# Last tokens' values by head in DRAM, their late output products moved, and a new instruction order, in a segment-recurrent attention kernel on Trainium2

## The chip, the cores and the metric

One Trainium2 chip, one of its cores. The metric is the device time of one execution in microseconds (us). The times before are 831.28, 831.71 and 833.63 us, median 831.71. Where a profile is read, it is one execution of the same program, recorded by the hardware profiler. The engines are named as the profile names them: PE is TensorE's matrix multiply, PEld its loading of weights (the stationary operand), DVE is VectorE, ACT ScalarE, POOL GpSimd, and SP the SyncE queue from which nearly all DMAs are issued.

## What is computed

Two attentions over the same 2048 tokens of width 512, mixed by a gate for each token. Branch A is recurrent: 64 segments of 32 tokens, each with 8 memory tokens ahead of it. The output of the memory rows of one segment is the memory of the next, so the 64 segments run strictly one after the other. Branch B has 32 heads of width 16, works in four blocks of 512 tokens and carries a state of keys and values from block to block.

```python
x, mem = A_x, A_mem0                        # [1,2048,512], [1,8,512]
for s in range(64):                         # branch A: H=32 heads, Dh=128
    h = concat([mem, x[:, 32*s:32*s+32]])   # 40 rows
    q, k, v = h @ Wq, h @ Wk, h @ Wv        # [32 heads, 40, 128] each
    p = softmax(where(mask, q @ k.T * 128**-0.5, -1e9))
    o = (p @ v) @ Wo                        # [40, 512]
    mem, a[s] = o[:8], o[8:]
b = infini_attention(x, B_wq, B_wk, B_wv, B_beta) @ B_wo
g = sigmoid(sum(x * gate_w))
out = g * a + (1 - g) * b
```

The mask lets every row see the memory and makes the 32 tokens causal. Therefore the last 8 of the 40 rows of a segment (the "last tokens", 24 to 31 of the segment) are seen by themselves alone. Neither their keys, queries and values nor their output products are on the way from one memory to the next.

## The kernel before

**The segment.** A tile of PE has 32 columns, so a segment's own work is done on 32 rows: the 24 first tokens and the 8 memory rows (`hT`, line 1420 fills the tokens, line 1317 the memory that the segment before left). Function `p_seg` issues, for each half `r` of 16 heads: the projections of q, k and v (`wproj`, its matmuls are line 1389), ScalarE or VectorE copies to SBUF, VectorE transposes in blocks of 32 x 32 (line 1445), the scores (1460), the exponentials, their sums (1483), the product with the values (1525), and the output product (`wo`, 1294) with a fold (1018) that gives the next segment's memory. Everything here hangs together in one chain, segment after segment.

**The last tokens.** The last 8 tokens of four segments make 32 rows together. Function `p_rest(j, kind, r)` projects them for four segments at once (`j` is a block of four segments, 0 to 15; six calls for each block). Their columns of `x` are gathered by POOL into `xr` (1342). Keys and queries are transposed by VectorE into `rem_k` and `rem_q` (1375). The values go through a staging buffer (`stg`, three of them in rotation, function `stage`) to DRAM (`rest_v`, line 1361, a row for each token), and `p_restload(s)` (1398) loads those of one segment into one of two buffers `rem_v`, so that a row of SBUF is a pair (head, token). They are used at line 1464 (keys and queries) and 1530 (the values, as a second part of the product 1525). Block 0 is brought to `rem_v` of segment 0 without DRAM, by a product with a matrix of ones and zeros, `spread`, which POOL makes at the start (lines 836 to 840).

**Late output products.** POOL collects the last tokens' attention outputs of four segments in `OTr` (1547), and function `p_orest(t)` multiplies them by `Wo` with the same `wo` (64 matmuls, eight groups of eight). Its result is stored as rows of `a_rows` in DRAM (1336). Function `p_tail(t)` loads 128 rows of `a_rows` (1267), adds branch B's output and stores the final rows (1279).

**Order.** All operations are created by functions that are called in the order of the keys given in `build` (`self.at(key, function, ...)`; a key of 52.3 is a little past segment 52). They are not issued in that order: `schedule` takes each engine's order word for word from the string `ORDER`, a compressed list of operation numbers for each of the five queues. The costs, loads and priorities in the calls were inputs of a planner that made this list. In the run they set only which PSUM banks are taken and which waits are left out as already implied. The waits themselves come from the reads and writes that each operation names (`reads`, `writes`), and each engine's queue is executed strictly in its order, so that an instruction that waits holds all behind it on its queue.

**Filler.** PE has nothing to do in many short moments of a segment's chain. The list puts there the matmuls that are not on the chain: the last tokens' projections and output products, branch B's projections, scores and values (1018, 1020, 1135, 1176), and the tails.

Of the kernel before, what the change touches and what calls it, by code (L numbers as in the profile page):

```python
# [8 lines left out]
ALU = mybir.AluOpType  # L9
AX = mybir.AxisListType  # L10
BF16 = mybir.dt.bfloat16
# [4 lines left out]
    "c-nPY2S8KT*FQHe$;%F5h*kvzgbJb-5f`;p+*<joRjYMxZCyxl*MZ_*EzVYL>#joGC_|-gl!_Mj!cn)N5E3BCecydA$;*3*pGr(#&OP^x-}#+$FT*v;w-P1BriC&|)l9G%"  # L16
    "s$dCNl9$dfOo!y$%Sq*U<KU-})t}r8g~OH`5C_L0IlpH{Zu60ErpZ%g?|dY)mVT8r{rR6&vufWz0XKitmNmTt@P2wmR^2Dcv_w$7^?_AAz2AA8e7FAFuxaq+6CJZ&>$@K7"
    "a`k4x;LhK`u7Fl2*3K}h-;zZ^CGUMQ3XHlb2NF6~pIm$7M7L^4SqPBZuB&lQes&dBOrNhbr&M-&?RW0{Gyur@9Aej5r1c*9z9FCBQ<MKYZ@AFnO|$d=EApZWoA|!<F)Pex"
    "qW?}XSAf!V?>@AKphu9`f7hJ7Uz&ji?#~&3*5!qbgAiq-=}NlHV5Lt-f!cbxIb3LaLi+iQZvQz&p|AIbJwvoMnT=8t&6;urZ7Elz{s9VecvjtqW{67b&Fei3-H%&F6RrAk"
    "jfrfpmX>0r1j@0$wIHITxRVJKaJ305d8}I2<rw+De-%R1j=?mTL2cAqEYPeVx*+<d_3sM{d94!w)=s1{WEMn~`p}h{>VJqxg;%LsZM+|HA3n{i^Rzw49p?HUNO*Z60pv2X"  # L20
    "%;xvh4-oZUFL|e`fYN=lZr6Dl8~`tP*J{I>Nlypld0Av;>O;_@;19Y=cme@NLy5M`zhX5&(w-+Nycz!jL<SydZ=;a5eCYy{7CsQUYA}u4u6+DSAArAjz1aZqIa@9vna$=`"
    "1v6&rsCP<}a>)dZs$${%eOq#QW3NG6NI~@0VWl>i%uGbfq)NI(Q~vvC3Z|q<P7;Z3Y{(qO0zBzlq-4Wj_(0D{m3`2C@G^rm^vVlpbgc`(!#$Sayy}eMeKw6Ic#&CT7QZTz"
    "IZ#m4lF<t49zer?>n)$T2y*jz-}(XU4sDueMhI!m+G-iR*CR7j00rLfewsz|o?ZJM@{G+aHi|M>t@0|<gJAHgG^y6kEC-PPP6S*A1lHd5d2t|svepYkTWoS|CCICZHxI*Y"
    "cOhy$BpevA7GNr`dSPU6)UL=u1ZV_2viD#pQJ7UW3Bcxw*54=amd;7h|1yb<tlojf($&)!lhv#NG{3nVs^p+zeb<wf$OI~>#kwYO<?M=;FwNyoje{-x4h|xCrPTLB(B1o8"
    "rEh^iMSZKO5#(1(4DdO(?~-X;{L4P1Y#941!K+QXew?W!pv$2OLy5*}(!kB0#M67kj5)mOspMx__uP6m>Qub?gRb?|j$klL%1KR-kVHV?&ZW0_YxBuZQ~mZaB>G4Vq;TjG"
    "P#_?t$X&L2lb<&|&gn?(iN1$W<5dlVnK;IVsO8lrmopaKB}*IL<Ai55?lbcMhg3>|BxP&n&7DYgZqz5$NLNMyJm<st8^GWZ!=Nu4QI-lOE=@Q<LPj<RWpg+a_dA617F^r`"
    "KlMr)MpgNgQk1sNgW!T_cxJ9(12*=LN4{@rSN=s1M`-8TlAU%;^-DO`PtQ@u7pEUUu+h6&CMoldd2P-BEvdK#ZSrC`c%N(wFr!^AEXuf?&Shi8c%Y?Vky_*>x)1&{8{C|?"
# [12 lines left out]
    "%dXODUOAuG7fA4=vs*KFmVzv9SVeY~QI#}jv1H?@mL!F`mKRwU3L{DFsQ2QfHrbXTUUG>=Y9@PHX`+43&xG12WN~OW(n___S4El^>#7`5rqf7Mo^lX*t(a~12-sD67?nXF"  # L40
    "q;r_W0z#d9E4ST48|6@BX-rN(#CA11y|B^Hu}cBr!MKPB6@LnL6B-szNL`%Vl5ITBm{sbDHe*B1W!463>&qlZ`V-6GP8IDmlt@YNs3CX^w_}My2Sz>7eiF|>2?x2%u{lv9"
    "Tzg=KQA4I<o!tf%(QNCU#p*8gVo{QoC{dSvnY@As+zC6`f{U<zPk*dFgr_2I9T#Lv<+@p*{tNtvP}>GsXa_WCl1UAP{cJKWJ**Mocc2+64&~y9aL8jTwdUC>iK;x(?jolw"
    "_zoMy<1m_Qq;@Y!(h%I(l}W}7ulF^bK5ENTW;f>HL@Xnb*aHjB4}B1P*Q-iT7FMXN3WU{3u~Rx^v!R~0meWSF8PA08C>;ke;yL@k*qp_eBZ5Uui4g}OkpRcnEZjg@pTLmy"
    "hh)eCH$Ic#0M+jPGTS@7Gx($;aKkSy#hgbU3{G_^3yHcZTl;09SN@bE;|hY*V3ttX&r!vk{!NMH>$lPyMmTj5K&g!l>|S%VASEW`ltZ#D_KH_o<L6v02R|dqy|CI9L!yeH"
    "z8B0GNO5Jv8A}R5tuef<L1|k28DNJ1=k|sE$iC1KXLT6O7nB{*$MA5<4rmsrB%+$*ILQGw9h(UvLt~l+{Q_9TDq_K<@um1Guz*|@_tMv?xEA{WVYGDe-sh_?NSm1?|LRIB"
    "^)c4`xK<zfpM8&%=gsM;9_esn^3(Bvi?1VJ!R_#2TglOC{JQb$G7n!cDd()18aXs65E{kKIG=ibkiHz$zYZ{`|CHH{hU3?7r0TDdPW#4E>s@`&-S^cML5NQ&w5U)Jf>9fD"
    "zA!uw3M{^OJDk2Z@`S2$SzUsDjCAl;E0-2VgMN=sH*?NVi-g9=Y6y8G#aClA2tH9ftjEf&nqZ(PsUG$YR}iGzwhZ;gcY7C6SDFX!MDY{XW{+2yZ->iJn_L5Jkru-1K3=6Y"
    "WqLEFu>qfLL*0s;6W2Sv_nDWy8>$K-Dhwuh;f}<Gv%)c5em3-8!SWm39tO%Q)Oa4O!ih_0>ihK<JLSYT1dAFI1s1vVR6I=W)C+=1(23Ej6M>q#=Gm+PJJWlq`gB)xeM<V7"
    "Z4P|hB5^Hl|8paYGz&VNK)uXIvo@s9i916q{x9Orr&4HhcFr2;mj?>74Ac~q`B)S+P2<-EzJ%JkN-RfhvkVtoN%4Zs&vT&h<`e`?D`^?RHZ4V0--upzyYcMbv^_J1wQYO^"
    "(<T~CTH%c)(yT7YU!XqlCqVMDALOts(Q966wSx3E+S^Kzt?~8=7In2!51|V3nJl{u?eMAAY6#oW{Nfw%$8C3CPFLKBpnq6`d#|s5{ZqMg;m(eKsQ>KJ6w51+0uIH7ez%&Y"  # L50
    "{{Aw2!=Mjv2x@!-#Hb}n28%lJJ5sh07~9k~_|M-UksgPx$NKH<``zc@orKA>pqsLmA}w|K<@F<e9dWz`nFukSy39aAD%F3VbF)drJ+s2r-~}EI@P{Rj9Ix8n{S5uJr=PZM"
# [12 lines left out]
    "WF>cwF#&(zB7X+6FKI7kY#lUq<8Lsq`pU}hTJP#HWM@Cg-roO9-<Q=c*R&Dee$uTk%v6_k+!O?x4jX@_18@Eq-+taNud9kT1$7-Tpj{1lRq=`Ru#IavEUl9idis5j_<Eys"
# [517 lines left out]
class Kernel:  # L582
# [1007 lines left out]
```

## Time and profile before

| | before |
|---|---|
| median of 3 runs | 831.71 us (831.28 to 833.63) |
| the profiled execution, device time | 832.18 us |
| its span, first to last instruction | 830.2 us |
| granted TensorE clock | 1.000 |
| loads of `rem_v` (line 1398) | 63 of 64 KB, issue 585 ns, landing 2.9 us (medians) |
| stores of `rest_v` (line 1361) | 28 of 128 KB from SP, 4 from ACT, issue 536 ns (SP, median) |
| VectorE transposes of last tokens (line 1375) | 64, 0.69 us each |

A line of the profile's list of groups gives line, engine, operation, output and inputs with their shapes, then the number of instructions, their busy time in us with the mean of one in ns, and the idle time of the engine just ahead of them with what ended it. In the table by stretches the columns are the stretch, its length, and for each engine the busy time with the number of instructions, then the granted clock, the mean share of the DMA engines, and GB/s. In the list of waits the three numbers are us in total, times, and the longest one. A line that begins with SPq is an instruction of the SP queue; its time is that of the issue, not of the transfer.

### The profile page before, as it was taken

The numbers are of one execution on the slowest core, as the hardware profiler recorded it, in microseconds if no ns is written. First come the engines' busy times: TensorE is split into PE (matmuls) and PEld (weight loads), VectorE is DVE, ScalarE is ACT, GpSimd is POOL, SyncE is SP. The second block draws the span as 40 slices with busy tenths as digits, with TensorE's granted clock in tenths as the row PEclk, the third lists the DMA queues.
The fourth block names the chain that finished last, engine by engine and source line by source line (L and its number), as shares of the span: only waits on it lengthen the run. The fifth ranks groups of instructions, "written<-read, shape, count | busy, mean of one in ns | idle before, by whom it ended". The sixth has DMA issues, their size and how long they took to land.

```text
span 830.2 us, 53252 instructions
## 1 busy us (share of the span) xinstructions
PE 805.0 (97%) x24462; PEld 520.7 (63%) x24462; DVE 623.3 (75%) x1417; ACT 557.7 (67%) x1264; POOL 256.8 (31%) x572
## 2 busy tenths in 40 slices
PE   8999999999999999999999999999999999998988
PEld 4446666666566666666666666666666666665655
DVE  4878667778778778677787787777777867777776
ACT  3667666777667766667666767677677666666663
POOL 3453221333232323322322422423313314333240
PEclk9999999999999999999999999999999999999999
DMA  9983101111111110211012111101111100001001
GB/s 345 412 249 61 45 17 39 39 45 23 47 27 28 39 26 19 50 34 44 25 39 43 39 27 32 41 18 32 32 36 33 40 25 12 21 19 26 10 22 36
DMA packets 71700, 45.62 MB, mean 55 GB/s; under 512 B 50046, under 2 KB 69942, under 8 KB 69942
## 3 DMA queue, kind: packets, MB, share of 16 engines
q1 hardware_dynamic: 70422, 41.18, 17.2%
q8 instruction: 192, 3.15, 1.6%
q10 hardware_dynamic: 1056, 1.05, 0.4%
q14 instruction: 30, 0.25, 0.1%
HBM read 30.72 MB, written 8.87 MB: 48 GB/s over the span
## 4 chain that ended last, share of the span: by engine, by line
PE 82%; DMA 6%; DVE 4%; ACT 4%; SPq 2%; issue 1%; POOL 0%; DVEq 0%; POOLq 0%
PE pb L1389 45%; PE pb L1294 16%; PE pb L1018 7%; DMA Wo_sb<-in_A_Wo_dram 4%; PE pb L1135 3%; PE pb L1525 3%; PE pb L1020 2%; PE pb L1176 2%; PE pb L1483 2%; PE pb L1460 1%; SPq L891 1%; DMA rest_v<-stg 1%; DMA wqB_sb<-in_B_wq_dram 1%; PE pb L1224 1%; ACT rc_sb L1489 1%
## 5 line engine op out<-in xcount | busy, mean ns | idle before, releaser
L995 ACT ACTIVATE st<-pb 128x512 bf16<-128x512 f32 (+2 forms) x309 | 147.0, 495 | 115.8 <-PE pb L1389 96.4
L1153 ACT ACTIVATE PTB<-pb 128x640 bf16<-128x640 f32 x240 | 159.3, 703 | 46.3 <-PE pb L1135 37.3
L1389 PE MATMUL pb<-Wv_sb,hT 128*32 128x512 bf16 x2048 | 160.0, 379 | 0.0
L1389 PE MATMUL pb<-Wq_sb,hT 128*32 128x256 bf16 (+1 forms) x3072 | 139.0, 308 | 0.4 <-DVE hT L1317 0.4
L1389 PE MATMUL pb<-Wk_sb,hT 128*32 128x512 bf16 x2048 | 134.1, 379 | 0.7 <-DVE phiK L1204 0.7
L1294 PE MATMUL pb<-Wo_sb,OT_sb 128*32 128x256 bf16 x4096 | 130.7, 273 | 1.3 <-issue 0.8
L1294 PEld LDWEIGHTS pb<-Wo_sb,OT_sb 128*32 128x32 bf16 x4096 | 101.3, 96 | 14.3 <-ACT OT_sb L995 2.2
L1389 PEld LDWEIGHTS pb<-Wq_sb,hT 128*32 128x32 bf16 x3072 | 83.6, 97 | 41.1 <-issue 1.1
L1159 POOL TENSOR_SCALAR_AFFINE_SELECT PTB<-PTB 128x512 bf16<-128x512 bf16 x120 | 77.0, 642 | 95.6 <-ACT PTB L1153 89.2
L1445 DVE STREAM_TRANSPOSE QT_sb<-st 128x256 bf16<-128x256 bf16 (+1 forms) x192 | 94.1, 508 | 9.2 <-ACT st L995 7.4
L1445 DVE STREAM_TRANSPOSE KT_sb<-st 128x512 bf16<-128x512 bf16 x128 | 89.3, 700 | 12.4 <-ACT st L995 10.3
L1494 POOL TENSOR_TENSOR PT_sb<-PT_sb,rc_sb 128x64 bf16<-128x64 bf16 x87 | 32.0, 368 | 212.1 <-ACT rc_sb L1489 203.6
L1389 PEld LDWEIGHTS pb<-Wk_sb,hT 128*32 128x32 bf16 x2048 | 57.1, 97 | 44.0 <-issue 2.1
L995 ACT ACTIVATE OT_sb<-pb 128x320 bf16<-128x320 f32 (+1 forms) x141 | 57.8, 426 | 35.9 <-PE pb L1530 34.5
L995 DVE CAST OT_sb<-pb 128x320 bf16<-128x320 f32 (+1 forms) x119 | 56.5, 481 | 22.6 <-PE pb L1530 21.7
L1389 PEld LDWEIGHTS pb<-Wv_sb,hT 128*32 128x32 bf16 x2048 | 51.8, 96 | 18.5 <-ACT st L995 0.2
L1317 DVE CAST hT<-pb 128x32 bf16<-128x32 f32 x63 | 12.0, 190 | 68.3 <-PE pb L1018 68.1
L1487 ACT ACTIVATE rc_sb<-pb 128x160 f32<-128x160 f32 x128 | 38.9, 304 | 32.7 <-PE pb L1483 31.8
L1468 ACT ACTIVATE PT_sb<-pb 128x224 bf16<-128x224 f32 x128 | 45.4, 356 | 14.7 <-PE pb L1464 9.5
L1491 DVE TENSOR_TENSOR PT_sb<-PT_sb,rc_sb 128x160 bf16<-128x160 bf16 x128 | 43.0, 336 | 14.6 <-ACT rc_sb L1489 13.6
L995 DVE CAST V_sb<-pb 128x512 bf16<-128x512 f32 x60 | 40.9, 683 | 7.5 <-PE pb L1389 6.7
L1489 ACT ACTIVATE rc_sb<-rc_sb 128x160 f32<-128x160 f32 x128 | 43.0, 336 | 3.3
(199 smaller groups left out, 1464.6 us busy)
## 6 DMA issues: line engine op xcount, KB each, us to landing
Wv_sb<-in_A_Wv_dram SPq DMA_DIRECT2D x4, 1024.0 KB, 10.7
Wk_sb<-in_A_Wk_dram SPq DMA_DIRECT2D x4, 1024.0 KB, 19.2
Wq_sb<-in_A_Wq_dram SPq DMA_DIRECT2D x4, 1024.0 KB, 25.6
Wo_sb<-in_A_Wo_dram SPq DMA_DIRECT2D x4, 1024.0 KB, 22.5
rem_v<-rest_v SPq DMA_DIRECT2D x63, 64.0 KB, 2.9
rest_v<-stg SPq DMA_DIRECT2D x28, 128.0 KB
a_rows<-ao SPq DMA_DIRECT2D x63, 32.0 KB
stg<-a_rows SPq DMA_DIRECT2D x15, 128.0 KB
```

The lines of the kernel that those rows point to most:

```text
L995: self.P.op(("act", "dve"), (lambda a: a.activation(dst, src(), ACT.Copy), lambda d: d.tensor_copy(dst, src())), reads=reads, writes=write ...
L1018: ins = pe.matmul(out[32 * c:32 * c + 32], lhsT[:, 32 * c:32 * c + 32], rhs, start=start, stop=stop, tile_position=(0, 32 * c), **kw)
L1153: P.op("act", (lambda dst=dst, src=src: lambda a: a.activation(dst, src(), ACT.Exp, scale=0.25))(), reads=[pair], writes=["%s%d_%d" % (nam ...
L1159: P.op("gp", (lambda pt=pt, ii=ii: (lambda g: g.affine_select(pt, pt, ([[0, len(ii)]] if len(ii) > 1 else []) + [[1, 128]], ALU.is_ge, 0.0 ...
L1294: ins = pe.matmul(pb[so.b][p0:p0 + 32, 0:256], tok(r, g, l), self.Wo[:, h, 256 * d:256 * d + 256], start=(r == 0 and g == 0 and l < 2), st ...
L1389: ins = pe.matmul(self.pb[sl.b][32 * g:32 * g + 32, 0:hi - lo], x[:, c, 0:32], cols, start=(c == 0), stop=(c == C - 1), tile_position=(0, ...
L1445: op("dve", (lambda dst=dst, src=src: lambda d: d.transpose(dst, src))(), reads=["st%d%s" % (i, tag)], writes=["%sT%d%s" % (kind, r, tag)] ...
L1468: op("act", lambda a: a.activation(PT[:, r, :], pb[rb.b][:, 0:224], ACT.Exp, scale=SCALE), reads=[rb], writes=["PT%d" % r, "PT%dr" % r], n ...
L1487: op("act", lambda a: a.activation(rc[:, r, :], pb[rb.b][:, 0:160], ACT.Ln), reads=[rb], writes=[rr], name="ln%d_%d" % (s, r), cost=t_act( ...
L1489: op("act", lambda a: a.activation(rc[:, r, :], rc[:, r, :], ACT.Exp, scale=-1.0), reads=[rr], writes=[rr], name="rc%d_%d" % (s, r), cost= ...
L1491: op("dve", lambda d: d.tensor_tensor(PT[:, r, 0:160], PT[:, r, 0:160], rc[:, r, :], ALU.mult), reads=[rp, rr], writes=[rp], name="nrm%d_% ...
L1494: op(("dve", "gp"), tuple((lambda e: e.tensor_tensor(rest, rest, late(rc[:, r, :]), ALU.mult)) for _ in range(2)), reads=[rp + "r", rr], w ...
```

## The change

Five things are changed.

1. **The values' place.** `rest_v` in DRAM is laid out by block of four segments, then head, then token, so that a pair (head, token of the eight) has the values of its four segments and two halves side by side. A store of 128 KB becomes four stores of 32 KB in pieces of 256 B. `rem_v` becomes one tile of two halves, and one load of 128 KB in pieces of 1 KB, made for every second segment, fills both. Blocks 0 and 1 (segments 0 to 7) keep rows of tokens, in `rest_v0`, with their stores on the ACT queue, and are loaded segment by segment, each half of the heads by a load of its own. The waits for `rem_v` are by half of the heads.
2. **The order of the 32 last tokens** of a block is now (token, segment) instead of (segment, token): in `xr`, in the transposes of line 1375, which write where the old ones did but in another order, and in `spread`, which needs one POOL operation less.
3. **Late output products.** Those of t = 12, 13, 14 get keys 57.5, 59.2 and 60.9 instead of 51.99, 55.99 and 59.99. For t = 13 and 14 the outputs are collected in two halves of `xT[0]`, which has no other use by then, so that `OTr` can hold t = 12 for longer. The last projections move by half a segment (j = 14) and one segment (j = 15).
4. **Figures of the planner** (`cost=`, `load=`) for some POOL copies and for the DMA transposes.
5. **`ORDER`**, the list of operation numbers for each queue, is new as a whole.

```diff
-        self.remv = [t("rem_v%d" % i, [128, 256]) for i in range(2)]
+        self.remv = t("rem_v", [128, 512])
-        self.rdram = nc.dram_tensor("rest_v", [self.NSEG * 8, H * self.E], BF16)
+        self.rdram = nc.dram_tensor("rest_v", [self.NSEG // 4, 32 * H * self.E], BF16)
+        self.rdram0 = nc.dram_tensor("rest_v0", [64, H * self.E], BF16)
+        late = [self.xT[0][:, 2 * i:2 * i + 2, :].rearrange("p c x -> p (c x)").rearrange("p (h q) -> p h q", q=32) for i in range(2)]
+        self.rest = [(self.OTr, ["OTr", "OTr0", "OTr1"])] * 13 + [(late[i], ["OTl%d" % i]) for i in range(2)] + [(self.OTr, ["OTr", "OTr0", "OTr1"])]
...
-            if s:
+            if s and (s < 4 * self.BYROW or s % 2 == 0):
                 self.at(s - 0.8, self.p_restload, s)
...
-                    self.at(4 * j - 3.7 + 0.5 * i, self.p_rest, j, k, r)
+                    self.at(4 * j - 3.7 + 0.5 * i + {14: 0.5, 15: 1.0}.get(j, 0.0), self.p_rest, j, k, r)
         for t in range(self.NT):
-            self.at(4 * t + 3.99 if t < 15 else 62.5, self.p_orest, t)
+            self.at({12: 57.5, 13: 59.2, 14: 60.9, 15: 62.5}.get(t, 4 * t + 3.99), self.p_orest, t)
...
-        op("gp", lambda g: g.affine_select(self.spread, self.spread, [[8, 4], [-1, 128]], ALU.not_equal, 1.0, base=0, channel_multiplier=1),
-           reads=["kT0"], writes=["kT0"], name="spread1", cost=0.75, prio=-100)
...
-            xr[:, :, :].rearrange("p c (s t) -> p c s t", t=8),
+            xr[:, :, :].rearrange("p c (t s) -> p c s t", t=8),
...
         if kind == "v":
-            dst = self.rdram[32 * j:32 * j + 32, 2048 * r:2048 * r + 2048].rearrange("t (g x) -> g t x", g=4)
-            P.dma(group, lambda s: s.dma_start(dst, st[:, 0:512]), reads=[rs], writes=["dv%d_%d" % (j, r)], name="rvst%d_%d" % (j, r),
-                  prio=prio, load=4.5 if j < 2 else 0.3, cost=0.5, eng="act" if j < 2 else "sp")
+            if j < self.BYROW:
+                dst = self.rdram0[32 * j:32 * j + 32, 2048 * r:2048 * r + 2048].rearrange("t (g x) -> g t x", g=4)
+                P.dma(group, lambda s: s.dma_start(dst, st[:, 0:512]), reads=[rs], writes=["dv%d_%d" % (j, r)], name="rvst%d_%d" % (j, r),
+                      prio=prio, load=4.5, cost=0.5, eng="act")
+            else:
+                dst = self.rdram[j].rearrange("(g l t r e) -> g t l r e", g=4, l=4, t=32, r=2)
+                for l in range(4):
+                    P.dma(group, lambda s, l=l: s.dma_start(dst[:, :, l, r, :], st[:, 128 * l:128 * l + 128]), reads=[rs], writes=["dv%d_%d_%d" % (j, r, l)],
+                          name="rvst%d_%d_%d" % (j, r, l), prio=prio + 0.001 * l, load=0.1, cost=0.4)
...
-        dst = self.rem[kind][:, 4 * (j % 2):4 * (j % 2) + 4, 128 * r:128 * r + 128].rearrange("p s (h k) -> p h s k", k=8)
-        P.op("dve", lambda d: d.transpose(dst, st[:, :].rearrange("p (h s k) -> p h s k", s=4, k=8)), reads=[rs],
+        dst = self.rem[kind][:, 4 * (j % 2):4 * (j % 2) + 4, 128 * r:128 * r + 128].rearrange("p s (h k) -> p h k s", k=8)
+        P.op("dve", lambda d: d.transpose(dst, st[:, :].rearrange("p (h k s) -> p h k s", s=4, k=8)), reads=[rs],
...
     def p_restload(self, s):
+        j, i = s // 4, s % 2
+        if j < self.BYROW:
...
+        src = self.rdram[j].rearrange("(p c) -> p c", c=1024)[:, 256 * (s % 4):256 * (s % 4) + 512]
+        self.P.dma(self.g_rem, lambda e: e.dma_start(self.remv[:, :], src), reads=["dv%d_%d_%d" % (j, r, l) for r in range(2) for l in range(4)],
+                   writes=["rem_v%d_%d" % (i, r) for i in range(2) for r in range(2)], name="rlv%d" % s, cost=0.45, load=0.3, ring=2.0, prio=self.now)
...
-            op("gp", lambda g: g.tensor_copy(self.OTr[:, :, 8 * (s % 4):8 * (s % 4) + 8], OT[:, :, :, SEG:L].rearrange("p g h k -> p (g h) k")),
+            own, names = self.rest[s // 4]
+            op("gp", lambda g: g.tensor_copy(own[:, :, 8 * (s % 4):8 * (s % 4) + 8], OT[:, :, :, SEG:L].rearrange("p g h k -> p (g h) k")),
```

More of the change, by code (lines that the diff above doesn't have):

```diff
@@ L82 @@
+    "K?Ezqtb2Ata)x1raos6|VlZ-;#iP@4+)HBM+QFUUfTK*f{)2?aP{_(iOLi>*T#W+fis0Dbu`7;TXt{jCl{ZJ>DNc8APFqMi1W78MLpx_c-1+u@5-Qgw"
 )
@@ L686 @@
     BYPE = 4
+    BYROW = 2
     WARM = 24
@@ L1077, in p_bphik @@
             P.dma(self.g_stg[b], lambda s: s.dma_start_transpose(st[:, :].rearrange("p (i f) -> p i f", f=128), KT8[:, :]), reads=["KT8_%d" % par],
-                  writes=["stg%d" % b], name="bkn%d" % u, cost=0.5,
-                  load=1.5, prio=prio - 0.4)
+                  writes=["stg%d" % b], name="bkn%d" % u, cost=1.3,
+                  load=0.9, prio=prio - 0.4)
             kn, rkn = lambda: st[:, :], "stg%d" % b
```

166 lines of the change are left out of this document (84 added, 82 removed).

## The prediction

> **What bounds the kernel now.** I read the profile page first (busy shares, slices, chain of waits).
>
> ```profile
> span 830.2 us, 53252 instructions
> PE 805.0 (97%) x24462; PEld 520.7 (63%) x24462; DVE 623.3 (75%) x1417; ACT 557.7 (67%) x1264; POOL 256.8 (31%) x572
> ...
> PE 82%; DMA 6%; DVE 4%; ACT 4%; SPq 2%; issue 1%; POOL 0%; DVEq 0%; POOLq 0%
> ```
>
> TensorE (PE) is busy 97% of the span and holds 82% of the chain that ended last. So the change can only win where PE stands idle: 830.2 - 805.0 = 25.2 us. Then the table of busy time by stretches shows where that is:
>
> ```profile
> core 0: us, PE busy (x) PEld busy (x) DVE busy (x) ACT busy (x) POOL busy (x), PEclk, DMA share, GB/s
> 60.00:745.00 685.00, 674.00 (x21062) 444.06 (x21063) 521.86 (x1178) 473.09 (x1072) 203.35 (x443) 1.00 0.14 33
> 745.00:815.00 70.00, 63.73 (x2088) 42.29 (x2084) 51.09 (x113) 44.13 (x106) 25.22 (x54) 1.00 0.08 20
> 815.00:830.00 15.00, 11.60 (x333) 7.16 (x325) 9.52 (x20) 6.34 (x19) 0.44 (x1) 1.00 0.14 39
> ```
>
> From 60 to 745 us PE idles 11.0 of 685 us (1.6%): the segments' own work and the filler (projections of the last tokens, late output products, the B part) cover nearly all of it. From 745 to 815 us it idles 6.27 of 70 us (9%): filler has run short, and the recurrence from segment to segment sets the pace. The VectorE copies that hand a segment's memory to the next (timeline) give that pace:
>
> ```profile
> 756.87 0.19 DVE L1317 CAST hT<-pb 128x32 bf16<-128x32 f32 x1 [1.62 <-PE pb L1018]
> 767.86 0.19 DVE L1317 CAST hT<-pb 128x32 bf16<-128x32 f32 x1 [1.49 <-PE pb L1018]
> 778.71 0.19 DVE L1317 CAST hT<-pb 128x32 bf16<-128x32 f32 x1 [2.18 <-PE pb L1018]
> ```
>
> 10.9 us per segment here; the first such copy is at 61.22 and the one at 745.87 is the 57th, so the full stretch runs at (745.87 - 61.22) / 56 = 12.2 us. A segment with filler costs some 1.3 us more than one with little.
>
> Last the queues, by line and by wait:
>
> ```profile
> L1398 SPq DMA_DIRECT2D rem_v<-rest_v x63: 567/585/1679, 57.8 to 798.7; - x63
> DMA to landing us min/median/max: 2.1/2.9/4.4
> ...
> L1361 SPq DMA_DIRECT2D rest_v<-stg x28: 513/536/593, 73.7 to 723.8; - x28
> ...
> PE pb L1389 <- DMA rest_v<-stg: 1.1, 3, 0.5
> ...
> SPq L1398 <- PE pb L1294: 173.5, 46, 8.7
> ```
>
> Nobody waits for the loads of `rem_v`; three times PE waited, 1.1 us together, for a store of last tokens' values to free its staging buffer. SP itself mostly stands and waits (173.5 us at the loads alone).
>
> **Part 1, values by head.** Removed: 63 loads and 28 stores from SP. Added: 28 loads of 128 KB, 14 loads of 32 KB (segments 1 to 7, one for each half), and 28 x 4 = 112 stores of 32 KB. The 256 B pieces only change sides: 63 x 256 = 16,128 before in the loads, 112 x 128 + 14 x 128 = 16,128 after, mostly in the stores; the 1 KB pieces stay 28 x 128. SP's issue time: before 63 x 0.585 + 28 x 0.536 = 51.9 us. After, with 0.35 to 0.585 for a large load (0.349 is the median of the row `stg<-a_rows`, also 128 rows of 1 KB) and 0.35 to 0.536 for a store: 54 to 85 us. That is 2 to 33 us more on a queue that waits far longer, so the first term is 0. Since the loads are waited for by nobody, fewer of them win nothing either.
>
> The store costs elsewhere: three staging buffers go round, and one is free only when its last store has landed. Three more issues ahead of that are 3 x 0.536 = 1.6 us. At the three places where PE already waited this is up to +4.8 us; where other work is put in the gap, 0; a gain is excluded. I take +0.5, because 25 of 28 stores cost PE nothing today.
>
> [...]
>
> The double load also moves a wait. Today the load for segment s overwrites what segment s-2 used and goes out some 0.3 us after that: it has about 22 us. Now an even load overwrites both halves, so SP waits for the second output product of s-1 (L1530, for instance ending at 754.03) and it must land before the first of s (763.78): 9.7 - 0.3 - 2.9 = 6.5 us of slack. Behind it in SP's queue stand stores of rows and the B weights' slices. I take 0 and price the case below.
>
> **Part 2, token order (k s).** The 64 transposes L1375 now write each element 512 B from the one before, where they wrote runs of eight. Their rows are 0.69 us, the same as K's transposes with whole rows (L1445, 0.70). No row has such a scatter. The nearest pair is the reduction L1100 that reads in steps of 68 B, 0.372 us for 136 elements, beside L1098 with 0.293 for as many: 0.58 ns an element, so 0 to +0.3 us each, 0 to 19 us of VectorE in all. VectorE idles a quarter of the span; I take 0. POOL loses one select of L836 before 57 us, under the weights' loading: 0. The edits of `cost=` and `prio` issue nothing.
>
> **Part 3, late output products.** The dense run of 64 matmuls of one such product takes 1.9 us (1.86 and 1.93 in the chain). That of t=12 now runs at 683 to 695 us and t=13 at 732 to 739; both get keys (57.5, 59.2 + 0.3) beyond 745. t=14 only moves inside the thin stretch. The six projections of the last block (0.9 us each) move by one segment, which takes two of them past 745. Crossing: 2 x 1.9 + 2 x 0.9 = 5.6 us. The full stretch gets shorter by that. The thin one has 6.27 us free, of which 1.6% of 70, 1.1 us, would stay open even at the full stretch's quality: 5.1 us can be filled. One product comes in eight pieces of 0.23 us and fits gaps of 0.5. Gain between 0 (the filler pushes the recurrence) and 5.1; I take two thirds, -3.4.
>
> **Part 4, the new order.** All queues follow the list in the string. Counted from it, ScalarE has 14 operations more, VectorE 19 fewer, POOL 4 more, PE as many. What it may win or lose between 60 and 745 is bounded by the idle time there: half of the 11 us either way, -5.5 to +5.5 (segments there take 10.8 to 13.9 us, so a list can be off by that much). I take -1.0, since VectorE, the second busiest, is relieved.
>
> **Sum.** 830.2 - 3.4 + 0.5 - 1.0 = 826.3 us of span. The profiled run took 832.18 in all, 2.0 beyond its span, and lies 0.5 over the median 831.71: 826.3 + 2.0 - 0.5 = **827.8 us**.
>
> **Rivals.** (0.3%, about what a measurement of this kernel can tell from no change, is 2.5 us.)
>
> B, *the order wins more*: the middle gives its whole 5.5 us. 830.2 - 3.4 + 0.5 - 5.5 + 1.5 = 823.3. For it: 11 us of idle and VectorE relieved. Against: the gaps there are mostly under 0.6 us.
>
> C, *filler for nothing*: the moved products lengthen the late segments by what they save earlier, and stores take 0.5 more. 831.71 + 0.5 - 1.0 = 831.2. For it: the recurrence has its own waits on VectorE and ScalarE in each gap; against: PE itself is idle in them.
>
> D, *late double loads* (the other side): SP reaches an even load more than 6.5 us after the buffers are free, and the segment waits. It happens today to single loads:
>
> ```profile
> 317.66 0.20 PE L1530 MATMUL pb<-PT_sb,rem_v 32*128 32x64 bf16 x4
> ...
> 329.49 1.23 SPq L907 DMA_TRANSPOSE xT<-in_A_x_dram  x1
> 330.76 0.58 SPq L979 DMA_DIRECT2D wvB_sb<-in_B_wv_dram  x1
> 331.39 0.62 SPq L1398 DMA_DIRECT2D rem_v<-rest_v  x1
> ```
>
> The buffer was free at 317.9 and the load went out 13.5 us later, behind a transpose that waited; another was 8.5 us late (270.0 to 278.45). With today's 22 us that was hidden. With 6.5 us the two would cost 7.0 + 2.0 = 9.0 us: 827.8 + 9.0 = 836.8. Against it: both stood behind `xT` transposes, of which only four run after 250 us (277, 329, 368, 417), and an order made for the short slack can put the load first. It decides from the first load that is over 6.5 us late.
>
> E, *scattered transposes*: +0.3 us each, half of them ahead of a transpose on the segment's path and half of that hidden: 16 x 0.3 = 4.8, so 832.6. [...]
>
> **Chances.** Forecast 0.40; B 0.15; C 0.12; E 0.08; D 0.25. Faster by over 0.3% (below 829.2): 0.40 + 0.15 = 0.55. Within: C and E, 0.20. Slower (above 834.2): 0.25. The forecast's own range is 825 to 829. The whole one, 822 to 837, leaves out part of B and the half of D with more late loads, under 0.2.
>
> **What would show it.** Right: PE idle between 745 and 815 us falls from 6.3 to about 3, with `Wo_sb,OTr_sb` products between 745 and 800; the handover copies still 10.9 to 11.5 us apart there, and the one of segment 57 some 5 us earlier. Part 1: no PE wait for `rem_v<-rest_v`; waits for `rest_v<-stg` at most 1.6 us together. Part 2: L1375's successor at 0.70 us. Wrong: late segments of 12 us (C), a PE wait that ends with `rem_v` (D), transposes at 1.0 us (E). A middle whose mean segment is not 12.0 to 12.2 us breaks part 4.

## The result, and the profile after

| | before | after |
|---|---|---|
| median | 831.65 us (831.28 to 833.63, 4 runs) | 911.99 us (909.32 to 913.74, 4 runs) |
| span of the profiled execution | 830.2 us | 910.2 us |
| granted TensorE clock in it | 1.000 | 0.994 |
| last tokens' transposes, 64, mean | 0.69 us | 2.46 us |

The ratio is 1.0955 (95% interval 1.0929 to 1.0981): the changed kernel is 80 us slower. The page of the changed kernel shows it in its busy times and in the chain of work that ended last (by engine, then by line). Its lines count some 4 to 16 more than before: 1385 was 1375, 1399 was 1389, 1461 was 1445, 1476 was 1460, 1321 was 1317.

```profile
span 910.2 us, 53292 instructions
...
PE 819.0 (90%) x24456; PEld 514.6 (57%) x24474; DVE 716.5 (79%) x1398; ACT 566.8 (62%) x1279; POOL 261.2 (29%) x576
...
PE 60%; DVE 30%; ACT 4%; issue 2%; DMA 2%; SPq 1%; POOL 1%; DVEq 0%; POOLq 0%; ACTq 0%
PE pb L1399 33%; PE pb L1298 11%; DVE rem_q L1385 8%; DVE rem_k L1385 8%; PE pb L1022 5%; PE pb L1139 2%; DVE KT_sb L1461 2%; DVE QT_sb L1461 2%; PE pb L1541 2%; DMA Wv_sb<-in_A_Wv_dram 2%; DVE OT_sb L999 1%; PE pb L1476 1%; PE pb L1180 1%; PE pb L1499 1%; PE pb L1024 1%
```

VectorE (DVE) held 4% of the chain and holds 30% now, and two groups of 32 instructions hold 8% each: the transposes of the last tokens' queries and keys. Their rows in the list of groups (count, then busy time and mean in ns, then idle time before them):

```profile
L1385 DVE STREAM_TRANSPOSE rem_q<-stg 128x512 bf16<-128x512 bf16 x32 | 78.9, 2464 | 2.4 <-ACT stg L999 2.2
L1385 DVE STREAM_TRANSPOSE rem_k<-stg 128x512 bf16<-128x512 bf16 x32 | 78.8, 2464 | 0.3
```

Before, the same instructions took 697 and 691 ns. That is 64 x 1.77 = 113 us more, added up over the instructions, for the same 512 elements in each partition; only the address of each written element differs. VectorE's busy time rises by less, from 617.4 us in the same program without the scatter (next section) to 716.5, by 99 us or 1.55 for each transpose, because the record of a scattered transpose overlaps that of the instruction behind it: below, `rem_k` starts at 314.97, lasts 2.49 us, and the next one starts at 317.09. How it reaches TensorE is seen in the waits of PE (us in total, times, longest), and in one place of the timeline, first VectorE's rows and then PE's:

```profile
PE pb L1399 <- DVE rem_q L1385: 13.0, 8, 2.7
PE pb L1476 <- DVE QT_sb L1461: 8.4, 9, 1.5
PE pb L1399 <- DVE rem_k L1385: 8.4, 7, 1.4
PE pb L1476 <- DVE KT_sb L1461: 5.8, 8, 1.3
```

```profile
314.97 2.49 DVE L1385 STREAM_TRANSPOSE rem_k<-stg 128x512 bf16<-128x512 bf16 x1
317.09 0.90 DVE L1461 STREAM_TRANSPOSE KT_sb<-st 128x512 bf16<-128x512 bf16 x1
317.90 1.32 DVE L1461 STREAM_TRANSPOSE QT_sb<-st 128x512 bf16<-128x512 bf16 x3
```

```profile
316.84 0.36 PE L1022 MATMUL pb<-hide_sb,neg_sb 128*32 128x224 bf16 x8
318.72 0.37 PE L1476 MATMUL pb<-QT_sb,KT_sb 128*32 128x40 bf16 x16 [1.51 <-DVE QT_sb L1461]
```

The transpose `rem_k` is not on the segment's chain. It stands in VectorE's queue ahead of the two transposes that are, and these start behind it, at 317.09 and 317.90: the scores (1476) start 1.5 us late, at 318.72, and what stands behind them in PE's queue starts later still (1480 at 318.91). The first kind of wait in the list is the other way in which it hurts: the projections that are filler (1399) wait for the transposes of last tokens and hold PE's queue meanwhile. (All 15 of these waits, 21.4 us, are at products with `xr`, the last tokens' columns.)

By the copies that hand over the memory (2nd, 57th, 63rd), the 80.0 us of span split into a start of +11.4 us (76.08 to 87.52), a full stretch of +63.1 (669.8 to 732.9, 12.2 to 13.3 us for a segment), a late stretch of +5.5 (67.7 to 73.2), and nothing at the end. The lower granted clock is not the cause: 0.6% of PE's 819.0 busy us would be 5 us, by an estimate.

### The profile page after: what moved, and what is told of

It is laid out like the page before. It is cut to its first block, busy times and chain, and to the rows that moved or that the text cites. A ratio compares the mean times of both kernels' runs of the same rounds, so it can differ in the third digit from the quotient of the medians.

```text
span 910.2 us, 53292 instructions
## 1 busy us (share of the span) xinstructions
PE 819.0 (90%) x24456; PEld 514.6 (57%) x24474; DVE 716.5 (79%) x1398; ACT 566.8 (62%) x1279; POOL 261.2 (29%) x576
## 4 chain that ended last, share of the span: by engine, by line
PE 60%; DVE 30%; ACT 4%; issue 2%; DMA 2%; SPq 1%; POOL 1%; DVEq 0%; POOLq 0%; ACTq 0%
PE pb L1399 33%; PE pb L1298 11%; DVE rem_q L1385 8%; DVE rem_k L1385 8%; PE pb L1022 5%; PE pb L1139 2%; DVE KT_sb L1461 2%; DVE QT_sb L1461 2%; PE pb L1541 2%; DMA Wv_sb<-in_A_Wv_dram 2%; DVE OT_sb L999 1%; PE pb L1476 1%; PE pb L1180 1%; PE pb L1499 1%; PE pb L1024 1%
## 5 line engine op out<-in xcount | busy, mean ns | idle before, releaser
L999 ACT ACTIVATE st<-pb 128x512 bf16<-128x512 f32 (+2 forms) x313 | 149.3, 496 | 122.5 <-PE pb L1399 93.5
L1399 PE MATMUL pb<-Wv_sb,hT 128*32 128x512 bf16 x2048 | 162.7, 379 | 0.9 <-DVE ao L1328 0.9
L1298 PE MATMUL pb<-Wo_sb,OT_sb 128*32 128x256 bf16 x4096 | 132.6, 273 | 5.4 <-DVE OT_sb L999 3.7
L1385 DVE STREAM_TRANSPOSE rem_q<-stg 128x512 bf16<-128x512 bf16 x32 | 78.9, 2464 | 2.4 <-ACT stg L999 2.2
L1385 DVE STREAM_TRANSPOSE rem_k<-stg 128x512 bf16<-128x512 bf16 x32 | 78.8, 2464 | 0.3
L1399 PE MATMUL pb<-Wv_sb,xr 128*32 128x512 bf16 x512 | 44.7, 386 | 12.7 <-DVE rem_q L1385 8.6
## 6 DMA issues: line engine op xcount, KB each, us to landing
Wv_sb<-in_A_Wv_dram SPq DMA_DIRECT2D x4, 1024.0 KB, 11.9
```

The costliest lines, as they stand in the source:

```text
L999: self.P.op(("act", "dve"), (lambda a: a.activation(dst, src(), ACT.Copy), lambda d: d.tensor_copy(dst, src())), reads=reads, writes=write ...
L1298: ins = pe.matmul(pb[so.b][p0:p0 + 32, 0:256], tok(r, g, l), self.Wo[:, h, 256 * d:256 * d + 256], start=(r == 0 and g == 0 and l < 2), st ...
L1385: P.op("dve", lambda d: d.transpose(dst, st[:, :].rearrange("p (h k s) -> p h k s", s=4, k=8)), reads=[rs], writes=["rem%s%d" % (kind, j % ...
L1399: ins = pe.matmul(self.pb[sl.b][32 * g:32 * g + 32, 0:hi - lo], x[:, c, 0:32], cols, start=(c == 0), stop=(c == C - 1), tile_position=(0, ...
```

## The experiments

All ratios are to the kernel before, run on the same chip beside it. In the code, `[...]` stands for an index that is left out.

**Runs of eight again.** The changed kernel, with the write of line 1385 in the old order and all else as changed.

```diff
-dst = self.rem[kind][...].rearrange("p s (h k) -> p h k s", k=8)
-d.transpose(dst, st[:, :].rearrange("p (h k s) -> p h k s", s=4, k=8))
+dst = self.rem[kind][...].rearrange("p s (h k) -> p h s k", k=8)
+d.transpose(dst, st[:, :].rearrange("p (h s k) -> p h s k", s=4, k=8))
```

> The changed kernel, except that the 64 transposes of last tokens write runs of eight elements again, as in the kernel before. Keys and queries of the last tokens so land with another token of their block; nothing else is different, and no operation is added or left out. Theory S (the scattered write alone makes the loss): the transposes fall from 2.46 to 0.70 us, VectorE loses 64 x 1.76 = 113 us of work, and the kernel comes out where the rest of the change puts it, 825 to 833 us. Rival O (the new order or the double loads cost much as well): the transposes fall as far, but the kernel stays at 850 to 890 us, with PE waiting for rem_v or for the new order's places.

Measured: 830.16 us (828.51 to 831.93, 12 runs), ratio 0.9973 (0.9961 to 0.9985). The whole loss is gone. Its busy times, its rows in the list of groups and its table by stretches (stretch, length, busy time of PE, PEld, DVE, ACT, POOL, clock, DMA share, GB/s):

```profile
PE 804.3 (97%) x24456; PEld 518.0 (62%) x24474; DVE 617.4 (74%) x1398; ACT 564.0 (68%) x1279; POOL 259.5 (31%) x576
```

```profile
L1385 DVE STREAM_TRANSPOSE rem_k<-stg 128x512 bf16<-128x512 bf16 x32 | 22.2, 694 | 0.3
L1385 DVE STREAM_TRANSPOSE rem_q<-stg 128x512 bf16<-128x512 bf16 x32 | 22.0, 689 | 2.2 <-ACT stg L999 2.0
```

```profile
60.00:745.00 685.00, 673.14 (x20989) 440.50 (x21003) 517.74 (x1166) 477.75 (x1088) 206.17 (x447) 1.00 0.14 33
745.00:815.00 70.00, 66.61 (x2191) 44.68 (x2184) 50.41 (x113) 45.43 (x107) 24.97 (x53) 1.00 0.09 24
```

These are the parts 1, 3 and 4 without part 2's cost: PE idles 11.9 us of the first stretch (11.0 before) and 3.4 of the second (6.3 before).

**The scatter alone.** The reverse: the kernel before, with only this write changed to the scattered order.

```diff
-dst = self.rem[kind][...].rearrange("p s (h k) -> p h s k", k=8)
-d.transpose(dst, st[:, :].rearrange("p (h s k) -> p h s k", s=4, k=8))
+dst = self.rem[kind][...].rearrange("p s (h k) -> p h k s", k=8)
+d.transpose(dst, st[:, :].rearrange("p (h k s) -> p h k s", s=4, k=8))
```

> The kernel before, except that the 64 transposes of last tokens write each element 512 B from the one before, as in the changed kernel. Keys and queries of the last tokens so land with another token; nothing else is different. Theory S: the transposes take 2.4 to 2.5 us and the kernel 900 to 920 us, as far from 831.7 as the changed one. Rival O: the transposes take as long, but in the old order most of the 113 us hides behind VectorE's idle quarter, and the kernel takes 840 to 870 us.

Measured: 924.51 us (923.51 to 926.29, 4 runs), ratio 1.1112 (1.1095 to 1.1129), somewhat above the 900 to 920 of theory S.

```profile
L1375 DVE STREAM_TRANSPOSE rem_q<-stg 128x512 bf16<-128x512 bf16 x32 | 78.9, 2466 | 1.4 <-ACT stg L995 1.0
L1375 DVE STREAM_TRANSPOSE rem_k<-stg 128x512 bf16<-128x512 bf16 x32 | 78.7, 2461 | 1.9 <-ACT stg L995 1.7
```

The same 2.46 us with the old values' store, the old late products and the old order. The scatter alone makes the loss, and is dearer here (92 us) than in the changed kernel, where taking it out won some 82 us (a ratio of 1.0955 against 0.9973). The order differs, and so does the granted clock: 0.983 in this profile against 0.994. By an estimate, 1.1% of PE's 825.6 busy us is 9 us, so the clock may be most of the difference; this was not tried.

**Rows by token.** The changed kernel with `rem_k` and `rem_q` laid out by token, so that a transpose writes one run of 512 elements; the readers (weight loads and matmuls at 1480, POOL's copies at 1438) step over 8 bytes instead.

```diff
-dst = self.rem[kind][...].rearrange("p s (h k) -> p h k s", k=8)
-d.transpose(dst, st[:, :].rearrange("p (h k s) -> p h k s", s=4, k=8))
+dst = self.rem[kind][...].rearrange("p (b s) x -> p b (s x)", b=2)[:, j % 2, 512 * r:512 * r + 512]
+d.transpose(dst, st[:, :])
-Kr, Qr = (self.rem[k][:, s % 8, :] for k in "kq")
+Kr, Qr = (self.rem[k][...].rearrange("p (b s) x -> p b (s x)", b=2)[:, s // 4 % 2, :].rearrange("p (x s) -> p s x", s=4)[:, s % 4, :] for k in "kq")
```

> The changed kernel with rem_k and rem_q laid out by token instead of by segment, so that the transposes write whole rows of 512; the readers (128 weight loads of keys for each half of the heads in four segments, and POOL's copy of the queries) then read with a step of 8 B. Nothing is left out. Theory S: transposes at 0.70 us and the time of e1 within 0.5%. Rival R (a step costs a reader as it costs a writer): the weight loads of rem_k rise from 93 ns to 150 or more, or POOL's copy from 0.42 us to over 0.8, and the kernel is 5 to 15 us above e1.

Measured: 830.44 us (828.81 to 832.18, 12 runs), ratio 0.9974 (0.9965 to 0.9984). The transposes are at 694 and 689 ns. The readers that step paid little: the weight loads of `rem_k` went from 93 to 107 ns, the matmuls from 190 to 196.

**The write by itself.** A program that does nothing but write 512 bf16 elements in each of 128 partitions, four times for each form: VectorE transposes that write four elements S elements apart and then the next four one element further on (`tp_sS`; the changed kernel does it with S = 256), or runs of n elements that lie 256 elements apart (`tp_rn`), plain copies on three engines (`cp` on VectorE, `ac` on ScalarE, `gp` on GpSimd), and stepped reads with plain writes (`rd` copies, `rdt` transposes).

```python
def jump(ap, S):   # four elements S apart, then the next four one element on
    return ap[:, 0:max(512, 4 * S)].rearrange("p (b s x) -> p b x s", s=4, x=S)[...]
def runs(ap, n):   # runs of n, the next run 256 elements on
    return ap[:, 0:1024].rearrange("p (s b k) -> p s b k", s=4, k=n)[...].rearrange("p s b k -> p b s k")
```

> Transposes and copies of 128 x 512 bf16 alone, four of each kind, with different steps between neighbouring elements of the output (s) or runs (r); the kernel computes nothing else. [...] Rival D (distance: what counts is the 512 B step, by banks or rows): steps of 8 to 32 elements stay near 0.70 us and the time rises with the step up to 256 elements. Rival T (only the transpose suffers): the plain copy with a step of 256 elements takes as long as with 1.

Measured, rows of the list of groups (after the bar: busy time in us, mean in ns, idle time):

```profile
L561 DVE STREAM_TRANSPOSE tp_s256x<-src 128x512 bf16<-128x512 bf16 x4 | 10.7, 2673 | 0.0
...
L561 DVE STREAM_TRANSPOSE tp_s8x<-src 128x512 bf16<-128x512 bf16 x4 | 9.8, 2440 | 0.0
...
L563 DVE COPY cp_s256x<-src 128x512 bf16<-128x512 bf16 x4 | 8.5, 2121 | 0.0
...
L561 DVE STREAM_TRANSPOSE tp_s4x<-src 128x512 bf16<-128x512 bf16 x4 | 5.0, 1256 | 0.0
...
L561 DVE STREAM_TRANSPOSE tp_r2x<-src 128x512 bf16<-128x512 bf16 x4 | 3.7, 918 | 0.0
...
L561 DVE STREAM_TRANSPOSE tp_r4x<-src 128x512 bf16<-128x512 bf16 x4 | 2.8, 691 | 0.0
L561 DVE STREAM_TRANSPOSE tp_s2x<-src 128x512 bf16<-128x512 bf16 x4 | 2.7, 684 | 0.0
L561 DVE STREAM_TRANSPOSE tp_s1x<-src 128x512 bf16<-128x512 bf16 x4 | 2.7, 682 | 0.0
```

The means of the copies must not be taken from this list. The timeline has the four of each kind one by one, and the first of VectorE's ran while GpSimd copied too:

```profile
20.57 3.85 DVE L563 COPY cp_s256x<-src 128x512 bf16<-128x512 bf16 x1
23.32 3.41 POOL L565 COPY gp_s256x<-src 128x512 bf16<-128x512 bf16 x1
24.05 3.04 DVE L573 COPY rd_s8x<-wide 128x512 bf16<-128x512 bf16 x1
...
44.79 0.26 DVE L563 COPY cp_s1x<-src 128x512 bf16<-128x512 bf16 x1
...
46.42 1.55 DVE L563 COPY cp_s256x<-src 128x512 bf16<-128x512 bf16 x1
47.56 0.71 DVE L573 COPY rd_s8x<-wide 128x512 bf16<-128x512 bf16 x1
48.16 0.60 DVE L573 COPY rd_s256x<-wide 128x512 bf16<-128x512 bf16 x1
```

The other three of each kind, with GpSimd and ScalarE done, agree within 0.04 us; their medians are used here. The transposes took as long beside GpSimd's copies as without (2.70 against 2.64 to 2.68 us with a step of 256), so their means stand.

The cost is not in the distance, as this run's rival D had it: steps of 8 to 32 elements took 2440 to 2599 ns, so 16 bytes (`s8`) cost nearly what 512 bytes (`s256`, 2673) cost. What counts is what lies closer together than that. Runs of four (691) and a step of 2 elements (684) took what a write in order took (682), pairs 918, a step of 4 elements 1256, a step of 8 elements 2440. It is not the transpose either: a plain VectorE copy goes from 0.27 us to 1.34 with a step of 8 and 1.55 with one of 256. Beside VectorE's transposes, ScalarE's copies went from 0.92 to 2.77 us and GpSimd's from 0.61 to 2.47 with a step of 256 (medians as well). And the read was cheaper than the write: the copy that reads with the same step of 256 takes 0.60, so the step costs 0.33 us at the reading side and 1.28 at the writing side.

**Half the dose.** The changed kernel with the keys' transposes writing in order (the keys laid out by token, read with a step), the queries' scattered.

```diff
+        if kind == "k":
+            dst = self.rem[kind][...].rearrange("p (b s) x -> p b (s x)", b=2)[:, j % 2, 512 * r:512 * r + 512].rearrange("p (h k s) -> p h k s", s=4, k=8)
-        Kr, Qr = (self.rem[k][:, s % 8, :] for k in "kq")
+        Kr = self.rem["k"][...].rearrange("p (b s) x -> p b (s x)", b=2)[:, s // 4 % 2, :].rearrange("p (x s) -> p s x", s=4)[:, s % 4, :]
+        Qr = self.rem["q"][:, s % 8, :]
```

> The kernel after with the keys laid out by token, so that the 32 transposes of keys write runs of four or more in order, while the 32 of queries stay scattered. Nothing is left out. This is the dose of the cost: half of the scattered writes. All theories have the transposes of queries at 2.46 us and those of keys near 0.69. If the loss goes by VectorE's time alone (each lump of 1.76 us delays the segment by the same share): half of 81.5 us, 830.4 + 41 = 871 us. If single lumps can be hidden and only pairs that fall on one another hurt: clearly less, 840 to 860. If one kind is nearer to the segment's path than the other: the keys' or the queries' share shows, 850 or 890.

Measured: 872.10 us (871.24 to 872.95, 2 runs), ratio 1.0492 (1.0463 to 1.0521).

The queries' transposes took 2461 ns, the keys' 694. Half the lumps, half the loss (871 was the figure for that): a lump of 1.77 us costs some 1.3 us at either dose (41.7 / 32 and 81.6 / 64, from 830.44). VectorE's busy time is 667.0 us here, so 84% of the added busy time comes through at half the dose (41.7 of 49.6) and 82% at the full one (81.6 of 99). In the profile of this run the start holds more than its half (the second handover at 86.5 us, against 78.0 with no scatter and 87.5 with all), the full stretch less (+29.5 of +67.5 us); by this one profile, the two kinds are not equally near to the chain in each stage.

**The start.** In the two kernels without scatter the second handover came at 78.0 and 78.4 us, 76.1 before, and ScalarE's waits show one that the kernel before has not (here of the kernel with rows by token):

```profile
ACT rc_sb L871 <- DMA st<-in_A_mem_dram: 2.2, 1, 2.2
```

Two lists were tried on the kernel with rows by token. One sends the small loads out ahead of the weights (SP's list), the other starts the work on `beta` later (ScalarE's and VectorE's lists).

```diff
 SP:      -Wv Wv Wv Wv  beta gate_w mem0   Wk ...
          +beta gate_w mem0   Wv Wv Wv Wv  Wk ...
```

> The kernel with rem_k and rem_q laid out by token (830.44 us, 0.9974 of before), with three entries of the SP list moved: the small loads beta, gate_w and mem0, which stand behind the four loads of Wv, go out ahead of them. Nothing is left out. In the kernel after and in the two mended ones ScalarE waits for these loads (2.2 to 2.6 us, once, at line 871, near 22 us), and TensorE is busy 7.5 to 7.8 us of 20 to 30 us where it was 9.8 before; the second handover is some 2.3 us later than before. Theory (the new order's start costs this, since it puts the work on beta three places earlier in ScalarE's list): the wait goes, TensorE is busy 9.5 us or more of 20 to 30, the second handover comes 1.5 to 2.3 us earlier, and the time falls by as much: 828.1 to 828.9 us, a ratio to before of 0.9947 to 0.9957. Rival 1 (the start is set by the arrival of the weights, the wait is only a sign of it): the wait goes, the second handover stays, ratio 0.997. Rival 2 (what the start gains is lost again where the filler runs short): second handover earlier, ratio 0.997.

```diff
 ScalarE: gB0 (exponential of beta)   moved three places on, behind three more exponentials of branch B
 VectorE: gB1 gB2 omgB, three of gP   moved behind the second copy of the last tokens' values
```

> The same base, the other way round: the loads stay where they are, and ScalarE's first operation on beta is moved behind the last of block 0's exponentials, and VectorE's six operations that follow from it behind the second copy of last tokens' values. Nothing is left out. Theory of the start: the wait for the small loads is gone, because they have landed by then; second handover 1.5 to 2.3 us earlier than in the base and 0.9947 to 0.9957 of before. Rival 1 (weights): no change, 0.997. Rival 2 (given back later): 0.997 with an earlier second handover. If it differs from the kernel with the loads first by more than 1 us, the place in the two engines' lists has a price of its own.

Measured: 830.78 us (828.12 to 833.05, 12 runs), ratio 0.9985 (0.9969 to 1.0001), and 831.06 us (827.36 to 832.85, 12 runs), ratio 0.9996 (0.9983 to 1.0009). ScalarE's wait was gone in the first and 0.2 us in the second, and nothing was won: PE was busy 8.4 (at a granted clock of 0.84) and 7.5 us of the stretch from 20 to 30 us (7.8 in their base, 9.8 before), the second handover came at 79.8 and 76.9 us. So taking away this wait does not bring the start back. What sets it was not found; in two more profiles of kernels with the base's lists the second handover came at 80.4 us without this wait and at 76.2 with 2.0 us of it, so the start also differs by as much from one execution to the next.

**The price of the late products.** In the kernel before and in the one with rows by token, the products of t = 12 and 13 leave out 50 of their 64 matmuls each; beside them, the second of these kernels once more as a base.

```diff
                         for d in range(2):
+                            if name in ("r12", "r13") and not ((r, g) == (0, 0) and l < 2 or (r, g) == (1, 3) and l >= 2 or (l, d) == (3, 1) and 0 < 4 * r + g < 7):
+                                continue
```

> What the late output products cost in their place. The kernel before, in which the output products of t = 12 and 13 leave out 50 of their 64 matmuls each (the rows of last tokens of segments 48 to 55 are incomplete); order, copies, stores and waits stay. 100 matmuls at 1.9 us for 64 are 3.0 us of TensorE. In the kernel before they run at 683 to 695 and 732 to 739 us, where TensorE idles 1.6%. Theory (part 3's: in the full stretch a matmul of filler costs its own time): the time falls by 2.7 to 3.0 us, a ratio of 0.9964 to 0.9968. Rival (the segments' chain sets the pace there too, filler fills gaps): by under 1 us, 0.9988 or more.

> The same 100 matmuls left out of the kernel with rem_k and rem_q laid out by token (0.9974 of before), where the two products run at 742 to 754 and 766 to 774 us, in the late stretch. Theory (part 3's: there the filler runs in idle time, for two thirds of it): the time falls by about 1.0 us, and the late stretch (57th to 63rd handover) from 69.8 to 68.8 us; ratio to before 0.9962. Rival C of the prediction (filler for nothing: late it lengthens the segments by as much as it takes): by 2.7 to 3.0 us, late stretch 66.8 to 67.1, ratio 0.9939 to 0.9942. If all of it is hidden: 0.9974 and 69.8.

> The kernel with rem_k and rem_q laid out by token, beside the two with thinner products on the same chip, as their base. Nothing is left out. As before: 0.9965 to 0.9984 of before, late stretch 69.8 us.

Measured: 830.38 us (828.85 to 834.46, 12 runs), ratio 1.0004 (0.9988 to 1.0020), thinned before; 829.78 us (827.26 to 833.64, 12 runs), ratio 0.9984 (0.9967 to 1.0000), thinned with rows by token; 830.42 us (827.86 to 831.86, 11 runs), ratio 0.9994 (0.9978 to 1.0010), its base. Taking 3.0 us of matmuls out of the full stretch wins nothing, at most 1.0 us by the interval; out of the late stretch it wins 0.8 us, within the error of the two intervals. The reason is seen in the segment of the kernel before that holds product 12. VectorE's handovers and PE's rows between the segment's output product and its fold, first in the kernel before, then thinned:

```profile
684.55 0.19 DVE L1317 CAST hT<-pb 128x32 bf16<-128x32 f32 x1 [1.93 <-PE pb L1018]
695.68 0.19 DVE L1317 CAST hT<-pb 128x32 bf16<-128x32 f32 x1 [1.36 <-PE pb L1018]
```

```profile
694.63 0.83 PE L1294 MATMUL pb<-Wo_sb,OTr_sb 128*32 128x256 bf16 x24
695.29 0.32 PE L1018 MATMUL pb<-fold_sb,st 128*32 128x16 f32 x16
```

```profile
682.67 0.19 DVE L1319 CAST hT<-pb 128x32 bf16<-128x32 f32 x1 [1.93 <-PE pb L1018]
693.80 0.19 DVE L1319 CAST hT<-pb 128x32 bf16<-128x32 f32 x1 [1.36 <-PE pb L1018]
```

```profile
692.75 0.50 PE L1296 MATMUL pb<-Wo_sb,OTr_sb 128*32 128x256 bf16 x6
693.41 0.32 PE L1018 MATMUL pb<-fold_sb,st 128*32 128x16 f32 x16 [0.16 <-ACT st L995]
```

The segment takes 11.13 us with 28 matmuls of the product in it and 11.13 with 6. The fold starts 0.66 us after the first of them either way, since it waits for ScalarE's copy of the output product (which ends at 695.23 in the kernel before, 0.06 us ahead of the fold). The idle time hardly shows: six matmuls spread over the gap count as 0.50 us busy, 24 as 0.83. The filler in this gap was free, though PE was busy for 10.98 of the 11.13 us.

A sum over the profile would mislead here: from the 2nd to the 57th handover the thinned kernel takes 667.1 us, the kernel before 669.8, and 2.7 us is what full price would give. But the four segments that hold the thinned products (51, 52, 55 and 56, counted by the handover that begins them) changed by +0.01, 0.00, +0.47 and -0.26 us. The difference lies in segments whose instructions are the same, and the ratio of 1.0004 shows nothing of it.

## Why the prediction was wrong, step by step

**Part 2, the step that failed.** The size "0 to +0.3 us each" and the choice of 0 for the scattered transposes. Measured: 1.77 us each, 113 us added up and 99 us of VectorE's busy time, 80 us of the whole. Two steps of it were wrong.

The price came from the nearest pair of rows, a reduction that *reads* in steps, 0.58 ns an element. The program with single forms comes near that figure for a read, (0.60 - 0.27) us / 512 = 0.64 ns, and shows that a scattered *write* is another thing: (1.55 - 0.27) us / 512 = 2.5 ns for the copy, (2464 - 694) / 512 = 3.5 for the transposes in the kernel. The row of reads was no bound for this write, and the upper end of the range should have stayed open.

The cover was wrong as well: "VectorE idles a quarter of the span". It still idles 21% in the slow kernel. Idle time in the mean hid little of the added work: the 1.55 us that one adds is longer than nearly all of VectorE's gaps (of 548 idle stretches between 60 and 820 us before, counted in the trace, 24 are longer), and what comes behind is late, as the place at 315 us shows. Of 99 us more of busy time some 82 came through, and half the dose gave half the loss: the cover was worth less than a fifth.

**Rival E** named the step that failed, at a chance of 0.08, and the wrong size, 832.6 us: its 0.3 us for each transpose came from the same row of reads, and 1.77 us was measured. Two rows of the program with single forms set the two orders side by side: runs of eight, as before, took 697 ns, a step of 256 elements, as changed, 2673.

**Part 1, values by head: +0.5.** Right in kind. In the kernel with runs of eight the 112 stores took 0.514 us each to issue (median, 0.536 was assumed), the 28 large loads 0.334, PE waited once for a store's staging buffer, 0.5 us (1.1 before), and nobody for `rem_v`. So rival D, the late double load, did not come. The upper end of the term, 4.8 us, did not come either. How long such a store takes to land no run shows.

**Part 3, late output products: -3.4.** The sign that it named came: PE's idle time from 745 to 815 us fell from 6.3 to 3.4 ("about 3"), and the handover of segment 57 came 3 us earlier (742.9; 5 were named). The size did not. By the handovers, segments 53 to 56 took 50.2 us before and 46.6 to 46.9 in the five profiles with the new order, no scatter and whole products; segments 57 to 62 took 67.7 before and 69.5 to 69.8. (In the second profile of the old order, that with the products thinned, they took 49.1 and 68.1.) So some 2 to 3.5 us were won and 1.4 to 2.1 lost, where the prediction counted 5.6 won and, with its two thirds, 2.2 lost. Its step "the full stretch gets shorter by that" took each moved matmul at its own busy time; the products alone, thinned in their old place, are worth 0 to 1.0 of 3.0 us. Whether the projections that moved with them or the new order around them made the rest, no run separates.

**Part 4, the new order: -1.0.** Not separated from part 3. Together, with part 1, they came to -0.5 to -2.2 us in time: 0.9973 and 0.9974 on one chip, 0.9994 on another, where -3.9 was forecast without any cost for part 2. Two profiles of one and the same kernel (rows by token) have the second handover at 78.0 and 80.4 us, and a full stretch of 665.4 and 662.2; differences of that size between single profiles were not read as effects, the start's 2 us among them.

**Rivals B and C.** Without the scatter the kernel lands between the forecast, 827.8 us, and C, "filler for nothing", 831.2 us: at 829.4 by the ratio on one chip (0.9973 of 831.65) and at C's figure by that on the other (0.9994). B's 823.3 us it did not reach.

The two repaired kernels (runs of eight, 830.16 us; rows by token, 830.44 us) are the best versions found, 82 us under the changed kernel. Over the kernel before the gain is 0.3% on one chip and not measurable on the other.

## What to carry to other kernels

When an edit changes only an access pattern, look at how each instruction writes its *output*: if not in runs of four bf16 elements or more (691 ns in the program with single forms) or with a step of two (684), measure that form by itself first (pairs took 918, a step of four 1256, of eight 2440), and let the side that reads do the stepping (107 instead of 93 ns for a weight load here, against 2464 instead of 694 for the write). Price a step by a row of the same kind: a stepped read did not bound a stepped write here (0.33 us against 1.28). And before counting on what moved filler gives back, thin it where it stands: the time that this wins is an estimate of what moving it away can win there (0 to 1.0 of 3.0 us here).

## What had not been expected of the hardware

- A VectorE transpose of 128x512 bf16 that writes with a step of 16 bytes took 3.6 times as long as one in order (2440 against 682 ns); a step of 512 bytes added a tenth to that (2673).
- Neither a step of 8 bytes (1256) nor pairs (918) came down to the time in order; a step of 4 bytes (684) and runs of four (691) did.
- With a step of 256 elements a read cost a VectorE copy 0.33 us more and a write 1.28, on top of 0.27 in order; reading with a step of 8 cost 0.44 more (0.71 in all).
- A VectorE copy and a GpSimd copy that ran at the same time lengthened each other (3.85 against 1.55 us, 3.41 against 2.47); VectorE's transposes beside GpSimd's copies did not (2.70 against 2.64 to 2.68, 2.47).
- ScalarE's and GpSimd's copies with scattered writes took longer as well (2.77 against 0.92, 2.47 against 0.61 us, measured beside VectorE's transposes).
